# Sums over keys moved from TensorE to VectorE, and their reciprocals spread by DMA, in an attention and feed-forward kernel

## Chip, cores and metric

One core of one Trainium2 chip runs the kernel. The metric is the device time of one execution in microseconds. The kernel before takes 1441.41 us (median of 3 runs, 1440.82 to 1441.47).

## What is computed

The reference is an attention block followed by a feed-forward block, in float32 (the two weight matrices arrive as float64 and are turned into float32 by the kernel):

```python
# q, k, v: (8 batches, 12 heads, 448 rows, 64)
q_n, k_n = rmsnorm(q, g_q), rmsnorm(k, g_k)       # over the last axis
attn = softmax(q_n @ k_n.T / sqrt(64))            # over the keys
x = (attn @ v)  ->  (3584, 768)                   # batch*row, head*64
h = x @ w_in                                      # 768 -> 2048, "L1"
out = relu(h)**2 @ w_out                          # 2048 -> 768, "L2"
```

The softmax's denominator is the sum over keys of the exponentials, one number for each head and query. It is this sum, and its reciprocal, that the change computes in another way.

## The kernel before, in words

**Units of work.** Attention runs over pairs of heads: 8 batches times 6 pairs, 48 pairs in all, numbered i. The feed-forward block runs over four spans of two batches (12 pairs). Both of its matrix products are done by Strassen's scheme with seven products (in the code A11, S2, S1, S3, A12, A22, S4).

**Stages.** (1) The first 12 pairs run alone, in `attention_alone` (L814), while other engines turn the weights into float32 blocks and write them to DRAM (`prepare` L541, called through `weights` L619 in small ticks). (2) Then, for each span: the first product (`first_product` L893), and the second product (`second_product` L949), beside which the attention of the next span's 12 pairs runs (`attention` L844). There are three such stages of attention beside L2; the last span's second product runs alone.

**Order.** The schedule is written by hand: each engine executes its instructions in the order of the Python code, and waits on semaphores. `attention` is a generator that yields three times in each pair's iteration; after each yield the loop at L1058 to L1061 takes a share of the second product's steps (nearly all of one matmul each; 180 in a span, 160 of them beside attention). So the order of one iteration i is: loads of pair i+3 (`load` L656), scores of pair i for two of its four blocks of keys (`scores` L742), the values of pair i-1 (`values` L767), the other two blocks of scores, `finish(i-1)`; yield; two additions; `combine_x(i-1)`, load of v; yield; `transposes(i+1)`, `norm(i+2)`; yield.

**Steps of one pair beside L2, by engine and line.**
- TensorE: scores L748 (keys on partitions, queries along the free axis), values L772, sums L783, second product L973. A matmul of float32 gives two records in the trace. The two heads' values, of 64 output partitions each, go to the two halves of one PSUM tile, and so do the two heads' sums.
- ScalarE: the exponentials L755 (into one of six places in turn), the scaling of the transposed q by the gains L729, the squares for the normalisation L707.
- VectorE: the four blocks of exponentials are added up (L761, three additions on 112 partitions x 896), then, after TensorE's sum over partitions with a matrix of ones (L783, into the PSUM tile `tot`, each sum on 64 partitions), the reciprocal of `tot` L796 and the product with the values L797. Further the transposes of the next pair's q and k in squares of 32 (L728), and the sums for the normalisation (L710 to L715). It also takes the second product's results out of PSUM (L984 to L992), transposes them (L961), and forms Strassen's combinations of x (L807 to L812) and, in the first span, of the activations (L887 to L891).
- GpSimd: the power -0.5 of the normalisation (L716) and the two multiplications with it (L718).
- SyncE issues all DMAs of this stage: eight loads of q and k for a pair (L666, in the four quarters of 32 columns), two of v (L683), the stored blocks of w_out (`sw`, L648, five buffers), and four stores of each output tile (L964). The loads of pair i+3 overwrite the places from which `norm(i+1)` reads q and k.

**PSUM.** Scores have two tiles of two banks (`ps_s`), values and sums one bank each (`ps_o`, tags "o" and "t"), the second product two banks (`ps_m`).

The transposed q and k of a pair have a single place (`qkT[:, 0]`), so L728 for pair i+1 runs after pair i's last scores, and pair i+1's first scores wait for L728 and L729.

Of the kernel before, what the change touches and what calls it, by code (L numbers as in the profile page):

```python
# [386 lines left out]
def attention_then_ffn_bounded(  # L387
# [65 lines left out]
    ps_m = ctx.enter_context(tc.tile_pool(name="ps_m", bufs=2, space=bass.MemoryType.PSUM))  # L453

    qk, qkT, ident, mhalf, gains, rstd0, _ = held
    ones = consts.tile([SP, D], F32, name="ones")
    gT = consts.tile([P, NFC, 2 * S], F32, name="gT")
    xT = consts.tile([P, 2, NPAIR, S], F32, name="xT")
    xC = consts.tile([P, 3, HC, S], F32, name="xC")
# [190 lines left out]


    pts = {}
    vs, probs, pavs, tots, accs, normed, rstds = {}, {}, {}, {}, {}, {}, {0: rstd0}
    places = []

    def load(i):  # L656
        if i < NAT:
# [84 lines left out]
    def scores(i, c):  # L742

        at = i % 2 if i < NAT else 0
        sc = ps_s.tile([SP, 2, 512], F32, tag="s", name="sc")
        for h in range(2):
            rows = slice(h * D, (h + 1) * D)
            nc.tensor.matmul(sc[:, h, 0:S], qkT[rows, at, 1, c * SP:(c + 1) * SP], qkT[rows, at, 0, :],  # L748
                             start=True, stop=True)
        pr = probs[i, c] = places[(NJ * i + c) % len(places)]  # L750
        if i < NAT:
            for h in range(2):
                nc.scalar.activation(pr[:, h], sc[:, h, 0:S], AF.Exp, scale=rstds[i][:, 1, 2 * c + h:2 * c + h + 1])  # L753
        else:
            nc.scalar.activation(pr, sc[:, :, 0:S], AF.Exp)  # L755

    def add_up(work, i, c):

        if c == 1:
            accs[i] = work.tile([SP, 2, S], F32, tag="acc", name="acc", bufs=1)  # L760
        nc.vector.tensor_tensor(accs[i], probs[i, 0] if c == 1 else accs[i], probs[i, c], ALU.add)  # L761

    def places_for(work, n):

        places[:] = [work.tile([SP, 2, S], F32, tag=f"pr{m}", name="pr", bufs=1) for m in range(n)]

    def values(i, pe_sums):  # L767
        pavs[i] = ps_o.tile([P, S], F32, tag="o", name="pav")
        for c in range(NJ):
            pr = probs.pop((i, c))  # L770
            for h in range(2):
                nc.tensor.matmul(pavs[i][h * D:(h + 1) * D, :], vs[i][:, h, c, :], pr[:, h, :],  # L772
                                 start=(c == 0), stop=(c == NJ - 1))
            if pe_sums:
                sums(i, pr, c == 0, c == NJ - 1)
        if not pe_sums:
            sums(i, accs.pop(i), True, True)

    def sums(i, pr, first, last):
        if first:  # L780
            tots[i] = ps_o.tile([P, S], F32, tag="t", name="tot")
        for h in range(2):
            nc.tensor.matmul(tots[i][h * D:(h + 1) * D, :], ones, pr[:, h, :], start=first, stop=last)  # L783

    def finish(i):

        b, hp = divmod(i, NPAIR)
        tot, pav = tots.pop(i), pavs.pop(i)
        x = xT[:, b % 2, hp]
        if i < NAT:  # L790

            nc.vector.reciprocal(x.rearrange("d (p j) -> d j p", j=NJ), tot.rearrange("d (j p) -> d j p", j=NJ))
            x = x.rearrange("d (p j) -> d p j", j=NJ)
            pav = pav.rearrange("d (j p) -> d p j", j=NJ)
        else:
            nc.vector.reciprocal(x, tot)  # L796
        nc.vector.tensor_tensor(x, pav, x, ALU.mult)  # L797
        del vs[i]

# [14 lines left out]
    def attention_alone():  # L814


        for i in range(NAT):
            if i + 3 < NAT:
                load(i + 3)
            scores(i, 0)  # L820
            scores(i, 1)
            if i + 2 < NAT:
                norm(i + 2)
            elif i + 1 == NAT:
                norm(NAT)
                load(NAT + 2)
            if i:
                combine_x(i - 1)
            load_v(i + 1)
            if i + 1 < NAT:  # L830
                transposes(i + 1)
            scores(i, 2)
            scores(i, 3)
            if i + 1 < NAT:
                take_transposes(i + 1)
            yield
            values(i, True)
            finish(i)
            if i + 1 == NAT:
                combine_x(i)  # L840
            if NAT <= i + 3 < NAT + 2:
                load(i + 3)

    def attention(work, first):  # L844


        last = first + 2 * NPAIR
        for i in range(first, last + 1):
            if i + 3 < min(last + 2, B * NPAIR):
                load(i + 3)  # L850
            if i < last:
                scores(i, 0)
                scores(i, 1)
            if i == first:
                yield
            if i > first:
                values(i - 1, False)
            if i < last:
                add_up(work, i, 1)
                scores(i, 2)  # L860
                scores(i, 3)
            if i > first:
                finish(i - 1)
            yield
            if i < last:
                add_up(work, i, 2)
                add_up(work, i, 3)
            if i > first:
                combine_x(i - 1)
            if i < min(last, B * NPAIR - 1):  # L870
                load_v(i + 1)
            yield
            if i + 1 < last:
                transposes(i + 1)
            if i + 2 < last:
                norm(i + 2)
            yield
# [15 lines left out]
    def first_product(work, span):  # L893
# [11 lines left out]
        for f in range(HF):  # L905
# [1 line left out]
            g11, g12 = gT[:, f, 0:S], gT[:, f, S:2 * S]  # L907
            g21, g22 = gT[:, HF + f, 0:S], gT[:, HF + f, S:2 * S]
            add = nc.vector.tensor_tensor
            sums = {}  # L910
            for i in range(7):

                into, rhs = {A11: ("pa", B11), S2: ("pb", T2), S1: ("pc", T1), S3: ("pd", T3),
                             A12: ("pa", B21), A22: ("pd", T4), S4: ("pc", B22)}[i]
                first = into not in sums
                if first and into == "pa":
                    if span == 0 and f:
                        sums[into] = ps_o.tile([P, S], F32, tag="ot"[f % 2], name="pa")
                    else:
                        sums[into] = ps_s.tile([P, 2, 512], F32, tag="s", name="pa")[:, 0, 0:S]  # L920
                elif first:
                    sums[into] = ps_m.tile([P, S], F32, tag="m", name=into)
                ps = sums[into]
                load_blocks(n + i + 5)
                for c in range(HC):
                    nc.tensor.matmul(ps, stream[n + i][:, c], rhs[:, c], start=first and c == 0,  # L926
                                     stop=c == HC - 1, skip_group_check=not first)
                if i == A11:
                    p1 = work.tile([P, S], F32, tag="p1", name="p1")
                    nc.scalar.copy(p1, ps)  # L930
                elif i == S2:
                    z = work.tile([P, S], F32, tag="z", name="z")
                    add(z, p1, ps, ALU.add)  # L933
                elif i == S1:
                    y = work.tile([P, S], F32, tag="y", name="y")
                    add(y, z, ps, ALU.add)
                elif i == A12:
                    activate(g11, ps)
                else:
                    g, x = {S3: (g22, y), A22: (g21, z), S4: (g12, z)}[i]  # L940
                    add(g, x, ps, ALU.add)  # L941
                    activate(g, g)
                if span and f and i in (S1, A22):
                    combine(f - 1, (int(i == A22),))
                if span and f == HF - 1 and i == S4:
                    combine(f)
                yield

    def second_product(work, span):  # L949
# [17 lines left out]

        p1s, c11s = {}, {}
        for j, (m, i) in enumerate(uses2):
            ps = ps_m.tile([P, S], F32, tag="m", name="ps")  # L970
            for c in range(HF):
                load_blocks(n + 5)
                nc.tensor.matmul(ps, stream[n][:, c % 4], rhs_of[i][:, c], start=c == 0, stop=c == HF - 1)  # L973
# [28 lines left out]
    load_v(0)  # L1002
    nc.vector.memset(clamp1, 1151.0)
    nc.vector.memset(clamp2, 255.0 * 2.0 ** 23)
    nc.vector.memset(ones, 1.0)

    def ahead(u, nxt):

# [8 lines left out]
    with tc.tile_pool(name="words", bufs=2) as spare["pool"]:  # L1017
# [4 lines left out]
        norm(1)  # L1022
        with tc.tile_pool(name="first", bufs=2, reuse_waits="tile") as work:
            places_for(work, NJ)
            weights(4)
            for u, _ in enumerate(attention_alone()):


                weights(min(EARLY, 8 + (EARLY - 8) * (u + 1) // (NAT - 1)))
                if u == NAT - 2:  # L1030
                    load_blocks(5)
        with tc.tile_pool(name="first_product", bufs=2, reuse_waits="tile") as work:
# [11 lines left out]
    for span in range(NSPAN):  # L1044
# [7 lines left out]
        with tc.tile_pool(name="second_product", bufs=2, reuse_waits="tile") as work:  # L1052
            rest = second_product(work, span)
            if more:
                places_for(work, NJ + 1)
                places.append(qkT[:SP, 1])
                total, done = HC * (7 * HF + 4) - 20, 0
                for u, _ in enumerate(attention(work, nxt)):  # L1058
                    while done < min(total, total * (u + 1) // (6 * NPAIR + 1)):
                        next(rest)  # L1060
                        done += 1  # L1061
            for _ in rest:
# [90 lines left out]
```

## Time and profile before

| | us |
|---|---|
| median of 3 runs | 1441.41 |
| the profiled execution | 1440.65 |
| its span in the trace | 1439.2 |
| TensorE busy | 1416.6 |
| VectorE busy | 804.4 |
| GpSimd busy | 534.1 |
| ScalarE busy | 449.8 |
| `tot` matmuls beside L2 (L783), busy | 33.2 |
| reciprocals of `tot` beside L2 (L796), 36 of 2951 ns | 106.2 |
| additions of exponentials (L761), 96 of about 1.09 us | 117.9 |
| attention beside L2, three stages | 275 to 480, 620 to 822, 964 to 1166 |

The profile is that of one execution. A group of instructions has a line of the source, an engine, an operation, a shape and a count, its busy time and its mean; then the time for which the engine stood idle just before these instructions and what released it. "PEld" is TensorE's weight load. The time of DMAs is not the issuing engine's: "SPq" shows how long SyncE took to issue, and a median tells how long after that the data had landed.

### The profile page before, as it was taken

How to read it: one execution, taken by the hardware profiler on the slowest of the kernel's cores; microseconds unless marked ns; L12 is line 12 of the kernel's file. 1: busy time of each engine (PE TensorE's matmuls, PEld its weight loads, DVE VectorE, ACT ScalarE, POOL GpSimd, SP SyncE). 2: the span in 40 equal slices, each digit the busy share in tenths (PEclk: the TensorE clock that was granted, in tenths of full speed). 3: DMA queues.
4: the chain of work that ended last, by engine and by line, in shares of the span. 5: the costliest groups of instructions: out<-in, count | busy, mean ns of one | idle time of the engine just before them, and what ended most of it. 6: DMA issues, size and time to landing. Idle time of an engine off the chain costs nothing.

```text
span 1439.2 us, 14368 instructions
## 1 busy us (share of the span) xinstructions
PE 1416.6 (98%) x4662; PEld 654.4 (45%) x4662; DVE 804.4 (56%) x1163; ACT 449.8 (31%) x652; POOL 534.1 (37%) x367
## 2 busy tenths in 40 slices
PE   7999999999999999999999999999999999999997
PEld 3433454444444455444444455544444445555553
DVE  6778888478767433456666633355666652332111
ACT  6887687423323012133232111223323201110000
POOL 5877688333442022523444012433334302221000
PEclk9999999999999999999999999999999999999999
DMA  8576898644445333344454342343544333333443
GB/s 236 171 219 162 301 383 315 180 87 107 101 89 102 97 88 88 97 98 106 98 109 88 89 102 87 93 115 81 109 98 103 76 83 87 87 88 102 106 113 70
DMA packets 423639, 180.37 MB, mean 125 GB/s; under 512 B 274820, under 2 KB 421508, under 8 KB 423556
## 3 DMA queue, kind: packets, MB, share of 16 engines
q1 hardware_dynamic: 419716, 178.91, 47.4%
q10 hardware_dynamic: 3712, 0.46, 0.2%
q8 instruction: 39, 0.64, 0.2%
q14 instruction: 44, 0.36, 0.1%
q0 software_dynamic: 128, 0.00, 0.0%
HBM read 146.28 MB, written 33.03 MB: 125 GB/s over the span
## 4 chain that ended last, share of the span: by engine, by line
PE 92%; DVE 4%; DMA 2%; issue 1%; ACT 1%; POOL 0%; SPq 0%; DVEq 0%; POOLq 0%; ACTq 0%
PE ps L973 32%; PE sc L748 11%; PE pav L772 10%; PE pd L926 10%; PE pa L926 10%; PE pc L926 10%; PE pb L926 5%; PE tot L783 4%; DVE acc L761 1%; DVE xT L796 1%; DMA sw<-w1s 1%; PE pt L734 1%; DMA words<-in_moe_w_out_dram 0%; ACT qkT L729 0%; DMA vt<-in_v_dram 0%
## 5 line engine op out<-in xcount | busy, mean ns | idle before, releaser
L716 POOL TENSOR_TENSOR half<-half,mhalf 128x28 f32<-128x28 f32 x36 | 173.3, 4813 | 343.1 <-DVE half L715 343.1
L973 PE MATMUL ps<-gT,sw 128*128 128x448 f32 x768 | 299.1, 542 | 0.0
L903 POOL TENSOR_TENSOR gT<-gT 128x448 f32<-128x448 f32 x96 | 94.9, 990 | 372.9 <-ACT gT L899 372.9
L973 PE MATMUL ps<-gC,sw 128*128 128x448 f32 x576 | 225.2, 542 | 0.0
L973 PEld LDWEIGHTS ps<-gT,sw 128*128 128x128 f32 x768 | 143.9, 190 | 149.9 <-issue 146.5
L748 PE MATMUL sc<-qkT 64*112 64x448 f32 x768 | 171.3, 564 | 6.4 <-ACT pr L753 3.8
L755 ACT ACTIVATE pr<-sc 112x896 f32<-112x896 f32 x120 | 104.7, 914 | 200.8 <-PE sc L748 200.8
L973 PEld LDWEIGHTS ps<-gC,sw 128*128 128x128 f32 x576 | 108.0, 190 | 112.3 <-issue 111.7
L926 PE MATMUL pa<-xT,sw 128*128 128x448 f32 x384 | 155.0, 540 | 0.8 <-DMA sw<-w1s 0.8
L772 PE MATMUL pav<-pr,vt 112*64 112x448 f32 x672 | 146.0, 549 | 1.3 <-PE sc L748 1.3
L899 ACT ACTIVATE gT<-gT 128x448 f32<-128x448 f32 x96 | 55.2, 575 | 285.7 <-DVE gT L941 285.6
L796 DVE RECIPROCAL xT<-tot 128x448 f32<-128x448 f32 x36 | 106.2, 2951 | 19.3 <-PE tot L783 19.3
L748 PEld LDWEIGHTS sc<-qkT 64*112 64x112 f32 x768 | 60.4, 173 | 105.5 <-issue 71.8
L926 PEld LDWEIGHTS pa<-xT,sw 128*128 128x128 f32 x384 | 72.8, 190 | 72.7 <-issue 72.2
L772 PEld LDWEIGHTS pav<-pr,vt 112*64 112x64 f32 x672 | 44.5, 137 | 89.3 <-issue 75.5
L926 PE MATMUL pd<-xT,sw 128*128 128x448 f32 x192 | 78.0, 542 | 0.6 <-DVE z L933 0.5
L729 ACT ACTIVATE qkT<-qkT,gains 128x448 f32<-128x448 f32 x36 | 24.1, 668 | 174.0 <-DVE qkT L728 174.0
L926 PE MATMUL pb<-xC,sw 128*128 128x448 f32 x192 | 77.7, 540 | 0.4 <-DVE xC L810 0.4
L926 PE MATMUL pc<-xC,sw 128*128 128x448 f32 x192 | 77.4, 539 | 0.0
L926 PE MATMUL pd<-xC,sw 128*128 128x448 f32 x192 | 77.4, 539 | 0.0
L926 PE MATMUL pc<-xT,sw 128*128 128x448 f32 x192 | 77.4, 539 | 0.0
L941 DVE TENSOR_TENSOR gT<-z,pd 128x448 f32<-128x448 f32 x32 | 19.9, 622 | 101.5 <-PE pd L926 101.4
(119 smaller groups left out, 1608.6 us busy)
## 6 DMA issues: line engine op xcount, KB each, us to landing
sw<-w1s SPq DMA_DIRECT2D x224, 192.0 KB, 2.4
sw<-w2s SPq DMA_DIRECT2D x168, 256.0 KB, 3.2
w1s<-gC SPq DMA_DIRECT2D x8, 1344.0 KB, 6.8
w2s<-gC SPq DMA_DIRECT2D x8, 1344.0 KB, 7.7
out_dram<-osb SPq DMA_DIRECT2D x184, 56.0 KB, 1.9
qk<-in_q_dram SPq DMA_DIRECT2D x144, 56.0 KB, 2.2
qk<-in_k_dram SPq DMA_DIRECT2D x144, 56.0 KB, 2.2
vt<-in_v_dram SPq DMA_DIRECT2D x72, 112.0 KB, 3.2
```

What stands on the lines that cost most here:

```text
L716: nc.gpsimd.tensor_tensor(half, half, mhalf, ALU.pow)
L729: nc.scalar.activation(qkT[:, 0, 0], qkT[:, 0, 0], AF.Copy, scale=gains[:, 0:1])
L748: nc.tensor.matmul(sc[:, h, 0:S], qkT[rows, at, 1, c * SP:(c + 1) * SP], qkT[rows, at, 0, :], start=True, stop=True)
L755: nc.scalar.activation(pr, sc[:, :, 0:S], AF.Exp)
L772: nc.tensor.matmul(pavs[i][h * D:(h + 1) * D, :], vs[i][:, h, c, :], pr[:, h, :], start=(c == 0), stop=(c == NJ - 1))
L783: nc.tensor.matmul(tots[i][h * D:(h + 1) * D, :], ones, pr[:, h, :], start=first, stop=last)
L796: nc.vector.reciprocal(x, tot)
L899: nc.scalar.activation(g, src, AF.Relu)
L903: nc.gpsimd.tensor_tensor(g, g, g, ALU.mult)
L926: nc.tensor.matmul(ps, stream[n + i][:, c], rhs[:, c], start=first and c == 0, stop=c == HC - 1, skip_group_check=not first)
L941: add(g, x, ps, ALU.add)
L973: nc.tensor.matmul(ps, stream[n][:, c % 4], rhs_of[i][:, c], start=c == 0, stop=c == HF - 1)
```

## The change

In the three stages of attention beside L2:
- The matmuls with ones are left out (they stay in the first 12 pairs). Instead `fold(i)` on VectorE transposes the added-up exponentials in squares of 32, sums along the free axis, brings the four groups of partitions onto one and adds them, takes the reciprocal of the 2 x 448 sums (now 32 partitions x 28), transposes them and has SyncE store them in DRAM (3.5 KB, `factors`, two buffers). `spread(i)` issues two DMAs that read them back, each onto 64 partitions, into the place of `xT` where `finish` then multiplies. `finish` has no reciprocal there.
- `attention` yields four times in an iteration instead of three. `spread(i-1)` follows `values(i-1)`; `fold(i)`, `finish(i-1)` and `combine_x(i-1)` stand between the second and the third yield of the iteration; `transposes(i+1)` and `norm(i+2)` follow the third.
- The second product uses the freed bank (`ps_o`, tag "t") for every third of its tiles.

In the first 12 pairs the first four ticks of the weights' preparation are taken after pair 0's first scores and `norm(2)`, instead of ahead of pair 0.

```diff
+    def fold(i):
+        NG = S // 32
+        acc, quarters = sums["acc"].rearrange("p h q -> p (h q)"), sums["quarters"]
+        turned = places[NJ * (i + 1) % len(places)].rearrange("p h q -> p (h q)")
+        nc.vector.transpose(turned, acc)
+        nc.vector.tensor_reduce(quarters[:, 0], turned.rearrange("p (n k) -> p n k", k=32), AX, ALU.add)
+        for n in range(1, 4):
+            nc.vector.tensor_copy(quarters[0:32, n], quarters[n * 32:(n + 1) * 32, 0])
+        square, turned = sums["square"][:, 0], sums["square"][:, 1]
+        nc.vector.tensor_reduce(square[:, 0:2 * NG], quarters[0:32].rearrange("p a n -> p n a"), AX, ALU.add)
+        nc.vector.reciprocal(square[:, 0:2 * NG], square[:, 0:2 * NG])
+        nc.vector.transpose(turned, square)
+        nc.sync.dma_start(sums["out"][i % 2], turned[0:2 * NG])
+
+    def spread(i):
+        b, hp = divmod(i, NPAIR)
+        for h in range(2):
+            nc.sync.dma_start(xT[h * D:(h + 1) * D, b % 2, hp],
+                              sums["out"][i % 2].rearrange("(h g) t -> h () (g t)", h=2)[h].to_broadcast([D, S]))
...
     def finish(i):
...
-        else:
-            nc.vector.reciprocal(x, tot)
         nc.vector.tensor_tensor(x, pav, x, ALU.mult)
...
     def attention_alone():
...
             if i:
                 combine_x(i - 1)
+            else:
+                yield
             load_v(i + 1)
...
-    def attention(work, first):
+    def attention(first):
...
             if i > first:
-                values(i - 1, False)
+                values(i - 1)
+                spread(i - 1)
             if i < last:
-                add_up(work, i, 1)
+                add_up(i, 1)
                 scores(i, 2)
                 scores(i, 3)
-            if i > first:
-                finish(i - 1)
             yield
             if i < last:
-                add_up(work, i, 2)
-                add_up(work, i, 3)
-            if i > first:
-                combine_x(i - 1)
+                add_up(i, 2)
+                add_up(i, 3)
             if i < min(last, B * NPAIR - 1):
                 load_v(i + 1)
             yield
+            if i < last:
+                fold(i)
+            if i > first:
+                finish(i - 1)
+                combine_x(i - 1)
+            yield
             if i + 1 < last:
                 transposes(i + 1)
...
-            ps = ps_m.tile([P, S], F32, tag="m", name="ps")
+            ps = (ps_o.tile([P, S], F32, tag="t", name="ps") if j % 3 == 2
+                  else ps_m.tile([P, S], F32, tag="m", name="ps"))
...
-            weights(4)
-            for u, _ in enumerate(attention_alone()):
+            for u, _ in enumerate(attention_alone(), -1):
...
-                weights(min(EARLY, 8 + (EARLY - 8) * (u + 1) // (NAT - 1)))
+                weights(min(EARLY, 8 + (EARLY - 8) * (u + 1) // (NAT - 1)) if u >= 0 else 4)
...
-                for u, _ in enumerate(attention(work, nxt)):
-                    while done < min(total, total * (u + 1) // (6 * NPAIR + 1)):
+                for u, _ in enumerate(attention(nxt)):
+                    while done < min(total, total * (u + 1) // (8 * NPAIR + 1)):
```

The rest of the diff gives `acc`, `quarters` and `square` their tiles (the rows of `acc` from 112 on, and the unused columns of `square`, are set by GpSimd once in each stage), makes the six places 128 partitions tall, moves the matrix of ones into the first stage's memory, and renames.

## The prediction, made before the changed kernel had run

> **What bounds the kernel now.** I read the engines' busy time, then the table by stages for the three stages of attention beside L2, then SyncE's waits, then the timeline of one pair in the middle stage.
>
> ```profile
> PE 1416.6 (98%) x4662; PEld 654.4 (45%) x4662; DVE 804.4 (56%) x1163; ACT 449.8 (31%) x652; POOL 534.1 (37%) x367
> ```
>
> The three stages (their length, then busy time of TensorE, its weight load, VectorE, ScalarE and GpSimd, with counts; granted clock, DMA share, GB/s):
>
> ```profile
> 275.00:480.00 205.00, 203.44 (x733) 87.55 (x729) 147.78 (x218) 58.95 (x74) 67.91 (x30) 1.00 0.45 97
> 620.00:822.00 202.00, 201.88 (x728) 87.08 (x726) 131.85 (x189) 58.68 (x73) 70.46 (x31) 1.00 0.45 98
> 964.00:1166.00 202.00, 201.88 (x727) 87.02 (x727) 131.84 (x189) 58.04 (x72) 69.73 (x31) 1.00 0.42 92
> ```
>
> TensorE is full in all three stages, at full clock. VectorE has 65 to 72%, GpSimd 35%. So what TensorE is spared would be gained, if nothing else becomes late. What could is not in busy shares but in waits:
>
> ```profile
> SPq L666 <- POOL qk L718: 176.5, 30, 10.8
> ```
>
> Thirty times SyncE's queue stands still, 176.5 us in all, until GpSimd has read the places that the next loads of q and k overwrite. Today nothing urgent is queued behind. One round of it, by the timeline:
>
> ```profile
> 716.08 1.17 DVE L728 STREAM_TRANSPOSE qkT<-qk 128x448 f32<-128x448 f32 x2
> 716.75 0.67 ACT L729 ACTIVATE qkT<-qkT,gains 128x448 f32<-128x448 f32 x1 [6.11 <-DVE qkT L728]
> 718.29 1.09 DVE L710 TENSOR_REDUCE half<-qk 128x28 f32<-128x896 f32 x1 [1.05 <-ACT qk L707]
> 718.71 1.76 PE L748 MATMUL sc<-qkT 64*112 64x448 f32 x8
> 720.45 0.18 DVE L715 TENSOR_SCALAR half<-half 128x28 f32<-128x28 f32 x1
> 720.71 4.80 POOL L716 TENSOR_TENSOR half<-half,mhalf 128x28 f32<-128x28 f32 x1 [10.53 <-DVE half L715]
> 725.58 1.84 POOL L718 TENSOR_TENSOR qk<-qk,half 128x448 f32<-128x448 f32 x2
> 726.55 1.89 SPq L666 DMA_DIRECT2D qk<-in_q_dram  x4
> 728.49 0.62 DVE L797 TENSOR_TENSOR xT<-pav,xT 128x448 f32<-128x448 f32 x1
> 728.54 1.99 SPq L666 DMA_DIRECT2D qk<-in_k_dram  x4
> 730.62 0.52 SPq L648 DMA_DIRECT2D sw<-w2s  x1
> ```
>
> Transposes and normalisation of one pair on VectorE, then 4.80 us of powers on GpSimd, then eight loads on SyncE until 730.62. TensorE's next scores come at 735.22: a pair takes 16.51 us (718.71 to 735.22).
>
> [...] a load of q is issued in 0.47 us and lands 2.2 us after issue (median). [...] after 3.19 us idle at 17.29 us eight score records took 3.33 us instead of 1.76; after 2.41 us idle at 13.14 us nothing was slow.
>
> **The change, part by part.** The sum is made against the profiled execution (1440.65 us, span 1439.2), 0.76 below the median.
>
> *Removed on TensorE.* Per pair one sum of two heads: in the timeline it begins at 706.95 and the next scores at 707.80, of which 0.10 us is the change of shape that stays: 0.75 us. 36 pairs: 27 us. A pair needs 16.51 - 0.75 = 15.76 us of TensorE.
>
> *Removed and added on VectorE.* Removed 36 reciprocals of 2.95 us. `fold`, not in the trace: transpose of 896 columns as the two of L728, 1.17; sum like L710, 1.09; three copies like L713, 0.6; sum of 28 groups of 4, 0.26 (reductions of 512 and 1024 elements took 0.68 and 1.22, so 0.145 + 112 x 0.00105); reciprocal of 28 columns at 2951/448 ns, 0.2; small transpose 0.15; together 3.5 to 3.6 (bounds 3.2 and 4.2). So 0.6 more per pair, of no weight by itself at 65%.
>
> *Added on SyncE.* Three issues a pair, some 0.5 us each. The store waits for `fold`; behind it stand blocks of L2's weights, which in the built order are used a pair later, and q/k loads, which come after GpSimd anyway: nothing. 8 MB more beside 180 MB at 45% DMA share: nothing.
>
> *The new wait.* In the built program's order the two broadcasts stand directly behind the eight loads L666 on SyncE, and `finish` waits for them on VectorE. Behind `finish` stand `combine_x`, the taking out of L2's tiles, and the next pair's L728, L710 to L715; TensorE waits for L728 and L729. That closes a ring, from one pair's L728 to the next:
> - L728 to L710, through ScalarE: 716.08 to 718.29, 2.21
> - L710 to the end of L715, 720.63: 2.34
> - power and first multiplication, until the first load is issued at 726.55: 5.92
> - eight loads issued, until 730.62: 4.07
> - first broadcast's issue 0.5, second's landing 2.7: 3.2. Landing is the unknown: loads of 56 KB took 2.2, those of v (112 KB, the same size) 3.2; I take the middle, bounds 2.2 and 3.7
> - `finish`'s product to the next instruction (728.49 to 729.03): 0.54
>
> Sum 18.3 us (17.7 to 19.4), longer than TensorE's 15.76, and it holds no matmul of L2 that could hide it. Each 448-wide VectorE instruction between `finish` and L728 adds 0.54. Counted in the built order: 19 in stage one (combinations of the activations), 11 in stage two, 6 in stage three: 10.3, 5.9, 3.2 us.
>
> *Rounds.* The first broadcast is in a stage's second iteration, the last transposes in the tenth after the first: ten rounds. The last stage loads nothing for pairs past 47: eight. The first L728 of a stage has no `finish` before it. It follows the end of the first pair's scores by 2.5 us of additions and 3.6 of `fold`; the next scores follow L728 by 1.35 (717.42 plus a hop), and TensorE gets there only after 9.9 (625.5 to 635.42). So a stage begins with 2.45 us in hand; in the first, four combinations (2.1) leave 0.35. Between the second and twelfth scores:
> - stage one: 183 + 10.3 - 0.35 = 192.9, before 167.7 (290.30 to 457.97): +25.3
> - stage two: 183 + 5.9 - 2.45 = 186.4, before 166.0: +20.4
> - stage three, eight rounds to the tenth scores: 146.4 + 3.2 - 2.45 = 147.2, before 133.6: +13.6. Its next two pairs save 1.5 and lose about as much, because three combinations stand behind `fold`.
>
> The two sums at each stage's end are saved: 3 x 1.5 = 4.5. Net +54.8 us. TensorE's idle 2.5 us per pair may halve its clock for a while (1.6 us more work): 17.4 is still under 18.3, cost nothing; without that cover 28 x 1.6 = 45.
>
> *Third bank.* No matmul of L2 waited for a bank: nothing; it covers tiles taken out late behind `finish`.
>
> *The moved ticks.* ScalarE now takes pair 0's first exponentials at 10.8, but then pair 2's squares (L693), ahead of the ticks and of the other exponentials. That pair was issued from 7.83 on and landed 7.9 us after (median): about 16.7. From there, with the trace's durations: L693 to the end of the first L580 3.0, two activations 1.9, four exponentials 2.1, two copies 1.1, two activations 1.9, then as before 4.0 (24.58 to 28.55) to pair 0's reciprocal: 30.7, before 28.55. Pair 1's values waited for that pair's product (32.26 in the trace), and TensorE is full from there on: +2.2. Bounds: 3 us gained if the loads land 5 us earlier, 4 lost.
>
> Sum: 1440.65 + 54.8 + 2.2 = 1497.7; plus 0.76: 1498 us.
>
> **Rivals.**
> 1. *The ring is longer* (1528 us): 64 readers of one line of DRAM land after 3.8 us instead of 2.7, 28 rounds of 1.1. For it: the landing is not in the trace. Against: only 3.5 KB are read again and again.
> 2. *The ring is shorter* (1462 us): loads issued or landing faster, 17.0 per round. Against: 0.47 us per issue in all of 80 loads.
> 3. *The ring doesn't bind* (1428 us, faster). One mechanism: the broadcast has landed before `fold` ends, some 6.1 us after a pair's last scores, so that only VectorE's queue sets L728. Then 27 us are saved, 2 lost at the start, and 12 where four combinations or three stand between `fold` and L728 (five pairs of stage one at about 1.5, the last ones at 1 to 2): 1441.4 - 27 + 2 + 12. It decides where a round falls below 16.3 us (18.3 - 57/28). For it: before, the loads were often all issued by 3 us after the scores (712.43 against 709.49). Against: there VectorE was early; once L728 is at the edge, everything behind it moves along.
> 4. *No change to be measured*: the ring near 16.3 by chance. That the sums are still on TensorE is excluded: the built program has none beside L2.
>
> **How the numbers follow.** Forecast 0.70 (1478 to 1520), longer 0.14, shorter 0.09, not binding 0.05, no change 0.02. A measurement of this kernel tells some 0.2% from no change. Faster 0.05, same 0.02, slower 0.93. The range: the ring's bounds, 28 x -0.6 and 28 x +1.1, and the start's give about 1474 to 1531.
>
> **What would show it.** Right: `tot` only in the first 12 pairs; SyncE's wait for L718 about as before; `finish`'s product released by the DMA of `xT`, two to four us idle each, 28 to 34 times; scores (L748) released by L729 with two to three us idle per pair; stages of about 220 us. Each hop of the ring can be read off. Wrong: `finish` running without a wait for a DMA, or TensorE full in the stages. At the start, L693 earlier than 16 us would refute the last term.

## The result, and the profile after

The changed kernel takes 1545.47 us (median of 4 runs, 1542.91 to 1548.23), the kernel before beside it 1441.44: a ratio of 1.0721 [1.0699, 1.0743]. The side was forecast, the size was not: 1498 us was predicted, and 1545 lies 14 us above the range's upper end.

Engines and granted clock (in tenths of full speed, by fortieths of the span) in the page of the changed kernel:

```profile
PE 1433.2 (93%) x4518; PEld 655.7 (42%) x4518; DVE 840.1 (54%) x1415; ACT 452.5 (29%) x652; POOL 544.6 (35%) x373
PEclk9999999999998999999999899999999999999999
```

TensorE has 144 matmul records fewer (the 36 pairs' sums), yet is busy 16.6 us longer, in a span of 1546.4 us instead of 1439.2. The three stages of attention beside L2, each now whole (length; busy time of TensorE, weight load, VectorE, ScalarE, GpSimd; clock; DMA share; GB/s):

```profile
279.40:524.00 244.60, 211.55 (x691) 89.00 (x691) 163.18 (x303) 60.55 (x74) 73.53 (x33) 0.93 0.41 93
662.40:903.00 240.60, 210.39 (x692) 88.62 (x692) 145.47 (x275) 59.67 (x73) 73.14 (x34) 0.94 0.42 95
1040.90:1276.00 235.10, 209.07 (x693) 88.44 (x693) 147.02 (x275) 59.97 (x73) 73.85 (x34) 0.94 0.40 93
```

Before, TensorE was full and its clock 1.00. Now it stands idle for 26 to 33 us in each stage, and some of the rest runs at half clock (0.50 from 754.12 to 757.45, below; the mean granted clock is 0.93 to 0.94). No other engine is nearly full: VectorE has 60 to 67%. So it is waits. SyncE's, and then the other engines' (who waits, for whom; us in all, times, longest):

```profile
SPq L666 <- POOL qk L718: 207.9, 30, 10.9
SPq L776 <- DVE square L775: 59.8, 21, 6.7
```

```profile
PE sc L748 <- ACT qkT L729: 89.3, 30, 5.2
DVE xT L821 <- DMA xT<-factors: 40.2, 18, 4.5
DVE ct L1020 <- PE ps L1003: 137.0, 31, 10.7
DVE y L1017 <- PE ps L1003: 44.0, 9, 6.5
```

TensorE's wait is the predicted one: scores wait for the scaling of the transposed q and k, 30 times. But only 18 of 36 finishes waited for the broadcast, where 28 to 34 had been foretold. And VectorE waits far longer than before for L2's tiles (the same two places had 91.3 and 16.2 us).

Where the time came from, by first scores of pairs (L748), in us:

| stretch | before | predicted | after |
|---|---|---|---|
| start of the first stage | 273.7 | +2.2 | 279.4 |
| stage one, second to twelfth scores | 167.7 | 192.9 | 205.2 |
| stage two, the same | 166.0 | 186.4 | 201.1 |
| stage three, second to tenth scores | 133.6 | 147.2 | 155.4 |
| stage three, tenth to twelfth scores | 32.5 | 32.5 | 39.7 |
| all the rest (changes alone) | | -4.5 | -0.1 |

The differences add up to the 107.2 us of the two spans. Two neighbouring rounds of stage two show what the sum had missed. The first, from one pair's transposes (L728) to the next pair's:

```profile
732.72 1.16 DVE L728 STREAM_TRANSPOSE qkT<-qk 128x448 f32<-128x448 f32 x2
737.35 4.79 POOL L716 TENSOR_TENSOR half<-half,mhalf 128x28 f32<-128x28 f32 x1 [11.95 <-DVE half L715]
742.22 2.79 POOL L718 TENSOR_TENSOR qk<-qk,half 128x448 f32<-128x448 f32 x2
744.14 1.89 SPq L666 DMA_DIRECT2D qk<-in_q_dram  x4
746.13 1.99 SPq L666 DMA_DIRECT2D qk<-in_k_dram  x4
748.08 0.20 DVE L775 STREAM_TRANSPOSE square<-square 32x32 f32<-32x32 f32 x1
748.16 1.13 SPq L782 DMA_DIRECT2D xT<-factors  x2
752.19 0.62 DVE L821 TENSOR_TENSOR xT<-pav,xT 128x448 f32<-128x448 f32 x1 [3.91 <-DMA xT<-factors]
752.73 1.16 DVE L728 STREAM_TRANSPOSE qkT<-qk 128x448 f32<-128x448 f32 x2
```

This is the predicted ring through SyncE: `fold` ends at 748.28 and VectorE then waits 3.91 us for the broadcast, which stood behind eight loads, which stood behind GpSimd. 20.0 us, where 18.3 (18.9 with this stage's instructions behind `finish`) was the sum. The next round:

```profile
754.12 3.33 PE L748 MATMUL sc<-qkT 64*112 64x448 f32 x8 [3.43 <-ACT qkT L729]
761.79 1.76 PE L748 MATMUL sc<-qkT 64*112 64x448 f32 x8
763.48 5.53 PE L1003 MATMUL ps<-gT,sw 128*128 128x448 f32 x14
765.12 1.09 DVE L760 TENSOR_TENSOR acc<-acc,qkT 112x896 f32<-112x896 f32 x1
767.21 1.13 SPq L782 DMA_DIRECT2D xT<-factors  x2
769.05 0.62 DVE L1020 TENSOR_TENSOR ct<-y,ps 128x448 f32<-128x448 f32 x1 [2.83 <-PE ps L1003]
770.12 1.10 DVE L768 STREAM_TRANSPOSE pr<-acc 128x896 f32<-128x896 f32 x1
773.69 0.20 DVE L775 STREAM_TRANSPOSE square<-square 32x32 f32<-32x32 f32 x1
773.83 0.57 DVE L821 TENSOR_TENSOR xT<-pav,xT 128x448 f32<-128x448 f32 x1
774.33 1.15 DVE L728 STREAM_TRANSPOSE qkT<-qk 128x448 f32<-128x448 f32 x2
```

Here `finish` waits for nothing: the broadcast was out early. What is late is `fold` itself. The sum was complete at 766.2, but VectorE's queue holds an L2 tile ahead of `fold` (L1020), TensorE begins on that tile only after its scores, and so `fold` starts at 770.12, 17.4 us after L728, and ends at 773.89. This is a second ring: L728, scores, values, scores, L2 tile, `fold`, `finish`, L728. It took 21.6 us, and TensorE's half clock after its idle 3.43 us (granted clock 0.50 from 754.12 to 757.45: 3.33 us for eight score records, not 1.76) lies on it.

### The profile page after: what moved, and what is told of

It reads as the page before. It is cut to its first block, busy times and chain, and to the rows that moved or that the text cites. A ratio compares the mean times of both kernels' runs of the same rounds, so it can differ in the third digit from the quotient of the medians.

```text
span 1546.4 us, 14545 instructions
## 1 busy us (share of the span) xinstructions
PE 1433.2 (93%) x4518; PEld 655.7 (42%) x4518; DVE 840.1 (54%) x1415; ACT 452.5 (29%) x652; POOL 544.6 (35%) x373
## 4 chain that ended last, share of the span: by engine, by line
PE 59%; issue 21%; DVE 7%; DMA 4%; POOL 3%; ACT 3%; SPq 2%; POOLq 0%; DVEq 0%; ACTq 0%
PE ps L1003 16%; PE pd L955 9%; PE pa L955 8%; PE pc L955 8%; PE sc L748 7%; PE pav L804 6%; PE pb L955 4%; PE tot L807 2%; POOL qk L718 2%; SPq L666 1%; DVE acc L760 1%; DMA sw<-w1s 1%; DMA xT<-factors 1%; DVE quarters L769 1%; DVE pr L768 1%
## 5 line engine op out<-in xcount | busy, mean ns | idle before, releaser
L748 PE MATMUL sc<-qkT 64*112 64x448 f32 x768 | 196.2, 634 | 91.1 <-ACT qkT L729 89.3
L804 PE MATMUL pav<-pr,vt 112*64 112x448 f32 x672 | 159.5, 589 | 7.4 <-ACT pr L753 4.2
L748 PEld LDWEIGHTS sc<-qkT 64*112 64x112 f32 x768 | 66.6, 190 | 198.4 <-ACT qkT L729 111.7
L760 DVE TENSOR_TENSOR acc<-acc,pr 112x896 f32<-112x896 f32 x60 | 74.8, 1247 | 66.8 <-ACT pr L755 64.1
L804 PEld LDWEIGHTS pav<-pr,vt 112*64 112x64 f32 x672 | 48.6, 150 | 116.0 <-issue 97.0
L718 POOL TENSOR_TENSOR qk<-qk,half 128x448 f32<-128x448 f32 x72 | 79.6, 1126 | 2.8
```

The source lines that it names most:

```text
L718: nc.gpsimd.tensor_tensor(qkn[:, s], raw[:, s], half[:, s * NG:(s + 1) * NG].rearrange("p g -> p g ()").to_broadcast([P, NG, 32]), ALU.mult)
L760: nc.vector.tensor_tensor(acc, probs[i, 0] if c == 1 else acc, probs[i, c], ALU.add)
```

## The experiments

The theory: two rings, through SyncE (S) and through `fold` (F), each longer than TensorE's 15.76 us per pair, and whichever is longer sets a round. The rivals: S alone, mis-sized; TensorE's half clock as the cause; the start; the third bank. All medians are of 4 runs unless another number stands there; the kernel before took 1441.3 to 1441.6 beside them. Edits are to the changed kernel.

**1. The start undone.** The first ticks of the weights go back ahead of the first 12 pairs.

```diff
-            else:
-                yield
...
-            for u, _ in enumerate(attention_alone(), -1):
+            weights(4)
+            for u, _ in enumerate(attention_alone()):
...
```

> The changed kernel with the first four ticks of the weights' preparation put back ahead of pair 0; all else as changed. In the changed trace the attention beside L2 begins 5.6 us later than before (279.38 against 273.74). Theory (the moved ticks make it late): 1540 us, 5 to 6 below the changed kernel, and the first stage begins at about 274 again. Rival (the start is late by chance or by the matrix of ones being set later): no change, 1545.

1541.64 us, 1.0691 [1.0673, 1.0709]: 3.8 us less than the changed kernel. The first stage began at 274.60 instead of 279.38. That is one execution of each, and this start varies: in the eight traces of changed kernels that keep the moved ticks it lies at 275.6 to 279.5 (mean 277.4), in the five that undo them at 273.6 to 276.4 (mean 274.8). So the start costs some 2.6 (by the means) to 3.8 us (by the medians). The loss lies elsewhere.

**2. S cut.** The broadcasts of pair i-1 are issued ahead of the loads, not behind them.

```diff
         for i in range(first, last + 1):
+            if i > first:
+                spread(i - 1)
             if i + 3 < min(last + 2, B * NPAIR):
                 load(i + 3)
...
                 values(i - 1)
-                spread(i - 1)
```

> The changed kernel with the two broadcasts issued at the top of the iteration, ahead of the eight loads of q and k, instead of behind them; VectorE's order is unchanged. This cuts the ring through SyncE's queue. Theory of two rings (the second goes from L728 through the next scores, the values, the exponentials, the additions, L2's tiles and fold to the next L728, and is lengthened only where TensorE has fallen to half clock): without the first ring [...] a pair takes 16 to 17 us, 1430 to 1455 us. Theory of the one ring, as predicted: everything is given back, 1420. Rival (fold on VectorE's path is the cause, and the broadcast only coincides): 1530 or more.

1502.48 us, 1.0429 [1.0412, 1.0446]. Waits of this run:

```profile
PE sc L748 <- ACT qkT L729: 59.9, 26, 4.3
DVE xT L821 <- DMA xT<-factors: 11.8, 3, 4.7
```

The broadcast is waited for 3 times, not 18, each time at a stage's end, with no scores behind it; yet scores still wait 26 times, and the time is 61 us over the kernel before. S alone as the cause falls: without it, F holds the rounds (15.4 to 21.6 us, with `fold` starting 10.7 to 16.2 us after L728 and `finish` directly behind it). Both expectations were too low, since F was taken for the shorter ring.

**3. No half clock.** Two matmuls more (1.5 us), whose result is overwritten, fill TensorE's idle time ahead of each pair's first scores beside L2.

```diff
+        for h in range(2 if i >= NAT and c == 0 else 0):
+            nc.tensor.matmul(sc[:, h % 2, 0:S], ident[:, 0:SP], gT[:, h, 0:S], start=True, stop=True)
```

> The changed kernel with two further matmuls of 128 x 112 x 448 on TensorE (1.5 us) directly ahead of each pair's first scores beside L2, into the tile that the scores then overwrite; they wait for nothing late. So TensorE has 54 us more work, in the place where it stands idle for 3 us on average. Theory of two rings with the half clock: the idle time falls to 1.5 us, the clock stays up, the rounds fall from 20.1 to about 18.7, 1500 to 1520 us, faster than the changed kernel although it does more. Rival (the clock has no part in it, a round is only SyncE's ring and longer than thought): 1545, unchanged, the work lies in the idle time. Rival (TensorE's work is on the path): 1545 + 54 = 1599.

1545.69 us, 1.0727 [1.0709, 1.0745]: no gain, though the clock over the run rose from 0.966 to 0.984 and only 8 of the 36 pairs' first scores were still slowed, where it had been 21.

```profile
PE sc L750 <- ACT qkT L729: 57.3, 24, 5.1
DVE xT L823 <- DMA xT<-factors: 50.2, 22, 4.8
```

Broadcast waits went up to 22 (50.2 us): where F became shorter, S took its place. So the half clock is not what decides, while S stands. How much it adds where F binds stays open, since the filling also takes TensorE's time.

**4. L728 taken out of both rings.** The next pair's transposes and normalisation go ahead of `finish` and `fold` in VectorE's queue, and `finish` ahead of `fold`.

```diff
             yield
-            if i < last:
-                fold(i)
-            if i > first:
-                finish(i - 1)
-                combine_x(i - 1)
-            yield
             if i + 1 < last:
                 transposes(i + 1)
             if i + 2 < last:
                 norm(i + 2)
             yield
+            if i > first:
+                finish(i - 1)
+                combine_x(i - 1)
+            if i < last:
+                fold(i)
+            yield
```

> The changed kernel with the next pair's transposes and normalisation on VectorE ahead of fold, finish and combine_x, instead of behind them; SyncE's order of broadcasts and loads is unchanged. L728 then waits neither for the broadcast nor for fold: both rings are cut. Theory (the order on VectorE is all that costs): TensorE is full in the three stages, 36 x 0.75 = 27 us are gained, 5.6 lost at the start: 1420 to 1430 us. Rival (the broadcast or its store is slow in itself, or SyncE's queue delays L2's weights): still above 1500.

1431.73 us, 0.9940 [0.9923, 0.9957]: all of the loss is gone and the kernel is a little faster than before, with the broadcasts still behind the eight loads and `fold` itself unchanged. SyncE even stands 169.7 us for `fold`'s result before it stores it, where it was 59.8 in the changed kernel, so that wait was not the loss either. What is left, in this run's waits:

```profile
PE pav L804 <- DVE xT L821: 9.0, 10, 2.1
PEld pav L804 <- DVE xT L821: 19.8, 15, 2.8
```

`finish` is now late for the single PSUM bank of the values.

**5. `fold` alone earlier**, directly behind the additions, SyncE's order unchanged.

```diff
                 add_up(i, 2)
                 add_up(i, 3)
+                fold(i)
...
             yield
-            if i < last:
-                fold(i)
             if i > first:
```

> The changed kernel with fold issued directly behind the last addition, one yield earlier, so that no tile of L2 stands ahead of it on VectorE; SyncE's order is unchanged. This shortens the second ring (fold behind a tile that TensorE finishes only 4 to 6 us after the scores) and leaves the first through SyncE. Theory of two rings: the first alone remains, rounds of 18.6 to 20, 1500 to 1525 us. Rival (the second ring is an effect of the first): no gain, 1545. Rival (the second is all): below 1460.

1535.64 us, 1.0647 [1.0629, 1.0665]: 9.8 less, a smaller gain than expected; experiment 6 shows why.

**6. Experiments 2 and 5 together.**

> Fold directly behind the last addition, and the broadcasts ahead of the eight loads on SyncE: the first ring cut, the second shortened to 1.4 + 6.5 + 2.7 + 3.8 + 0.55 us plus what stands between finish and L728, 15 to 17 us against TensorE's 15.76. Theory of two rings: 1425 to 1450 us. Rival (a third delay is hidden behind the two): 1480 or more.

1488.3 us, 1.0320 [1.0303, 1.0338]. Far off what was expected. The timeline of a round says why:

```profile
752.12 2.52 PE L1003 MATMUL ps<-gC,sw 128*128 128x448 f32 x6
754.68 0.62 DVE L1020 TENSOR_TENSOR ct<-p,ps 128x448 f32<-128x448 f32 x1 [4.42 <-PE ps L1003]
755.21 2.46 DVE L760 TENSOR_TENSOR acc<-acc,pr 112x896 f32<-112x896 f32 x2
757.70 1.11 DVE L768 STREAM_TRANSPOSE pr<-acc 128x896 f32<-128x896 f32 x1
```

The tile that VectorE waits for (4.42 us) stands ahead of the last two additions, as it does in some rounds of the changed kernel too (5.16 us at 409.10 there): after the first yield of an iteration L2's steps are queued, and the additions follow the yield. Moving `fold` to the additions didn't take the tile out of F.

**7. The next pair first, and everything else.** Transposes, then `fold`, directly behind the additions; after the yield `norm`, then `finish`; with 1 and 2.

```diff
                 add_up(i, 3)
+            if i + 1 < last:
+                transposes(i + 1)
+            if i < last:
+                fold(i)
...
             yield
-            if i < last:
-                fold(i)
+            if i + 2 < last:
+                norm(i + 2)
             if i > first:
                 finish(i - 1)
                 combine_x(i - 1)
             yield
-            if i + 1 < last:
-                transposes(i + 1)
-            if i + 2 < last:
-                norm(i + 2)
             yield
```

> The next pair's transposes directly behind the last addition, then fold; the normalisation ahead of finish; broadcasts ahead of the loads; the first ticks back ahead of pair 0. Everything that was late is then early. Theory: TensorE is full in the three stages, 27 us less of 1441.4: 1412 to 1420 us.

1439.01 us (18 runs), 0.9981 [0.9974, 0.9989]; some 20 more than expected. The values wait for `finish` (22.1 us, and 42.7 of their weight loads), which frees their bank: it stands behind `fold` and `norm`, and starts 17.8 us after a pair's first scores, where it was 16.3 in 4 (medians).

**8. The same with two banks for L2.**

```diff
-            ps = (ps_o.tile([P, S], F32, tag="t", name="ps") if j % 3 == 2
-                  else ps_m.tile([P, S], F32, tag="m", name="ps"))
+            ps = ps_m.tile([P, S], F32, tag="m", name="ps")
```

> As e7_next_first_all, with two banks for the second product instead of three. Theory (no matmul of L2 waits for a bank): the same as e7 within 2 us. Rival (tiles are taken out late behind fold on VectorE, and the third bank covers it): 5 to 20 us more than e7.

1438.3 us (10 runs), 0.9973 [0.9964, 0.9983], the intervals of 7 and 8 overlap: in the order of 7 the third bank is worth nothing that can be measured. In the changed kernel's own order it was not tried.

**9. F shortened, S as it was.** The last two additions and `fold` go ahead of the first yield, so that no tile stands before them.

```diff
                 scores(i, 2)
                 scores(i, 3)
-            yield
-            if i < last:
                 add_up(i, 2)
                 add_up(i, 3)
+                fold(i)
+            yield
...
             yield
-            if i < last:
-                fold(i)
             if i > first:
```

> The changed kernel with the last two additions and fold issued on VectorE directly behind the pair's scores, ahead of the first yield, so that no tile of L2 (which VectorE would wait 3 to 5 us for) stands ahead of them; SyncE's order unchanged. In e5 and e6 such a tile still stood ahead of the additions. Theory (ring through SyncE, and a second ring whose size is VectorE's wait for L2's tile): the SyncE ring alone remains, rounds of 18.3 to 19.5, 1500 to 1525 us. Rival (the tile's wait is not the term): as e5, 1535.

1527.91 us, 1.0613 [1.0584, 1.0642], 3 above the expected stretch. The broadcast is now waited for 22 times, not 18, and such a round is S alone:

```profile
738.67 1.11 DVE L768 STREAM_TRANSPOSE pr<-acc 128x896 f32<-128x896 f32 x1
742.25 0.20 DVE L775 STREAM_TRANSPOSE square<-square 32x32 f32<-32x32 f32 x1
746.78 0.62 DVE L821 TENSOR_TENSOR xT<-pav,xT 128x448 f32<-128x448 f32 x1 [3.83 <-DMA xT<-factors]
```

`fold` has ended by 742.45, and `finish` waits 3.83 us for the broadcast. This is what the prediction had described. The kernel takes 30 us more than the prediction said; but F is not gone from it: in a third of the rounds `finish` still follows `fold` without a wait for the broadcast.

**10. Experiments 2 and 9 together**: S cut, F shortened.

> As e9_adds_early, and the broadcasts ahead of the eight loads on SyncE as in e2. Theory (these two are all): the second ring shrinks to some 15 to 16.5 us, TensorE's 15.76 decides, 1422 to 1440 us. Rival (the tile's wait is not the term): as e6, 1488.

1464.56 us, 1.0162 [1.0142, 1.0183]. Better than either alone, but 25 above the expected stretch. One round:

```profile
707.99 2.84 DVE L760 TENSOR_TENSOR acc<-acc,pr 112x896 f32<-112x896 f32 x2 [2.54 <-ACT pr L755]
710.93 1.11 DVE L768 STREAM_TRANSPOSE pr<-acc 128x896 f32<-128x896 f32 x1
714.64 0.57 DVE L1013 TENSOR_TENSOR p<-p,ps 128x448 f32<-128x448 f32 x1
715.14 0.60 DVE L821 TENSOR_TENSOR xT<-pav,xT 128x448 f32<-128x448 f32 x1
715.67 1.15 DVE L728 STREAM_TRANSPOSE qkT<-qk 128x448 f32<-128x448 f32 x2
```

No wait for a tile or a broadcast is left in it, and from the last L728 (699.38) it still takes 16.3 us: scores, values, scores, additions, `fold` and `finish` in a row. Even the bare ring F, 15.4 to 17.8 us at full clock in stages two and three, is mostly longer than TensorE's 15.76. So L728 should not stand behind `fold` here.

**11. The best version.** Experiment 10, with the next pair's transposes between additions and `fold`, `finish` ahead of `norm`, and the start undone.

```diff
...
                 scores(i, 3)
-            yield
-            if i < last:
                 add_up(i, 2)
                 add_up(i, 3)
+                if i + 1 < last:
+                    transposes(i + 1)
+                fold(i)
+            yield
             if i < min(last, B * NPAIR - 1):
                 load_v(i + 1)
-            yield
-            if i < last:
-                fold(i)
             if i > first:
                 finish(i - 1)
                 combine_x(i - 1)
             yield
-            if i + 1 < last:
-                transposes(i + 1)
             if i + 2 < last:
                 norm(i + 2)
+            yield
             yield
...
```

> As e10, with the next pair's transposes between the additions and fold, finish ahead of the normalisation, and the first ticks back ahead of pair 0. Theory: TensorE waits for nothing in the three stages, 27 us are gained: 1412 to 1422 us. Rival (VectorE's queue, at some 85% of a pair of 15.76 us, makes something else late): 1425 to 1440.

1411.44 us, 0.9787 [0.977, 0.9803]: the fastest of all, 30 us under the kernel before. Its page and one iteration on VectorE:

```profile
PE 1389.8 (98%) x4518; PEld 643.5 (46%) x4518; DVE 839.6 (59%) x1415; ACT 450.8 (32%) x652; POOL 555.6 (39%) x373
```

```profile
699.97 0.63 DVE L728 STREAM_TRANSPOSE qkT<-qk 128x448 f32<-128x448 f32 x1
700.88 0.65 DVE L728 STREAM_TRANSPOSE qkT<-qk 128x448 f32<-128x448 f32 x1 [0.28 <-POOL qk L718]
701.45 1.07 DVE L768 STREAM_TRANSPOSE pr<-acc 128x896 f32<-128x896 f32 x1
704.99 0.20 DVE L775 STREAM_TRANSPOSE square<-square 32x32 f32<-32x32 f32 x1
705.12 0.57 DVE L821 TENSOR_TENSOR xT<-pav,xT 128x448 f32<-128x448 f32 x1
```

L728 runs as soon as the additions behind the scores are done, `fold` and `finish` behind it, where nobody on TensorE waits for them. TensorE is full again: eleven pairs of stage two follow each other in 174.1 us, 15.83 each, where it was 182.6 and 16.60 before.

**12. Experiments 4, 2 and 1 together**, the other way to take L728 out.

> e4_next_first (1431.7) with the broadcasts ahead of the loads and the first ticks back ahead of pair 0. In e4 VectorE waited six times for the broadcast, 23.3 us, and TensorE 29 us in all for finish. Theory: 4 us from the start and up to 15 from these waits, 1412 to 1427. Rival (finish is late for fold's and L2's tiles' sake): 1428, the start's 4 us alone.

1422.93 us, 0.9872 [0.9855, 0.9888], inside the expected stretch. Between 4 and 11: `finish` behind `norm` is still late for the values' bank (7.7 us, and 17.2 of weight loads).

The runs that matter, side by side (us):

| | S as changed | S cut |
|---|---|---|
| F as changed | 1545 | 1502 |
| F shortened | 1528 | 1465 |
| L728 out of F and S | 1432 (4) | 1423 (12), 1411 (11) |

Experiments 11 and 12 also have the start undone. Cutting S is worth 43 with F as it was, and 63 with F shortened; shortening F is worth 18 with S as it was, and 38 with S cut. Each saves more once the other is out of the way, as it must where the longer of two sets each round. With neither in L728's way, the sign turns.

## Why the prediction was right or wrong

**TensorE's share: right.** 0.75 us per pair was to be saved, 15.76 to be left. Experiment 11 shows pairs of 15.83 us in the mean, 15.76 the commonest; its span is 27.0 us shorter than that of the kernel before (1412.2 against 1439.2), its median 30. Third bank at nothing: not contradicted (8, in another order).

**The ring through SyncE: right in its path, too short in its terms.** Hop by hop from L728, predicted and then as the changed kernel's rounds had it:
- first load issued: 10.47; 10.45 in some rounds, 11.42 in others. In the latter GpSimd's first multiplication L718 lay beside the additions L760 on VectorE: the two multiplications take 2.79 above (742.22) instead of 1.84. In this trace L718 takes 0.94 us (median) and up to 1.90, L760 1.09 and up to 1.87. The 17 of 72 L718 that took over 1.0 us each overlapped an L760, and the 21 of 108 L760 that took over 1.15 each overlapped an L718; 17 more L718 overlapped an L760 and took no more than 0.94. Why some are lengthened and others not is not shown. The trace of before had shown it too (lines below): two multiplications in 2.69 us beside an addition of 1.39, while the round used for the sum, with 1.84, was one without
- broadcasts issued: 14.54; 14.48 or 15.44
- `finish`: 17.74; 17.9 to 19.7. Issue 0.58 each and landing 2.8 us (2.6 to 4.7) instead of 0.5 and 2.7

```profile
707.49 2.69 POOL L718 TENSOR_TENSOR qk<-qk,half 128x448 f32<-128x448 f32 x2
707.99 1.39 DVE L761 TENSOR_TENSOR acc<-pr 112x896 f32<-112x896 f32 x1 [4.92 <-PE tot L783]
```

With `fold` earlier (9) the kernel takes 1527.91, 30 above the prediction. In its trace the start is no part of that (275.6, 1.9 late where 2.2 was predicted). The rounds of the three stages took 25.4 more than the sum had, and all the rest 3.6 more. The longer hops are in the 25.4, and so are the rounds of F that are left in 9; how they share it was not worked out.

**The step that failed** is in rival 3: that `fold` ends "some 6.1 us after a pair's last scores", and so lies beside the ring. In the second round above the scores ended at 763.5 and `fold` at 773.9, 10.3 later; over the 36 pairs it was 6.4 to 10.3, the median 9.1. The 6.1 were additions and `fold` as if VectorE's queue held nothing between them. But what stands in a queue ahead counts: an L2 tile, whose matmuls TensorE only starts behind those scores; in stage one also four combinations of 0.6 each (287.8 to 290.2). Where the prediction's sum has L2's tiles, behind `finish`, they cost 0.54 us each with no wait for their matmuls; the tile ahead of `fold` above waited 2.83. So `fold`, whose 0.6 us of work more per pair were "of no weight by itself", closed a second ring. What experiment 9 takes out of that ring is worth 17.6 us with S as it was (1545.47 - 1527.91), and 37.9 where S is cut (1502.48 - 1464.56). That 17.6 and the 30 are the 47 us that the prediction was short.

**TensorE's half clock at no cost: the reason was too narrow, the cost is open.** The 17.4 us under 18.3 looked at TensorE's work alone; on F the scores are a hop, and from L728 to their end a round needs 9.4 to 10.9 us at half clock instead of 8.0. Experiment 3 found no gain from a higher clock while S stands, as predicted; its share on F isn't settled.

**Stage ends: wrong.** Each stage's last two sums were to save 1.5 us. The twelfth pair's first scores ran at half clock (granted 0.52 and 0.54 in stages two and three: 3.24 us, not 1.76), which takes back 1.5; in all 2 us were lost from there on. The rounds before a stage's second scores gave 2.2 back, so that the last row of the table is -0.1, not -4.5. And the last two pairs of stage three, put at nothing, lost 7.3: F binds there, with no load of q or k left on SyncE.

**The start: right in its cause, near in its size.** Lines of the changed kernel:

```profile
17.41 1.06 ACT L693 ACTIVATE qk<-qk 112x1024 f32<-112x1024 f32 x1 [5.35 <-DMA qk<-in_k_dram]
22.90 2.28 PE L804 MATMUL pav<-pr,vt 112*64 112x448 f32 x4 [4.22 <-ACT pr L753]
31.18 2.95 DVE L818 RECIPROCAL xT<-tot 128x448 f32<-128x448 f32 x1
```

L693 at 17.41 (predicted 16.7) and the reciprocal at 31.18 (30.7) are as worked out: ScalarE sits idle 5.35 us for the loads of pair 2. Left out was that TensorE then waits 4.22 us in the middle of pair 0's values and goes on at half clock (granted 0.50). The first stage started 5.6 late in this execution, not 2.2; the means over the traces (1) are 2.6 apart, and undoing it gave back 3.8.

**The range** took in the bounds of the landing and the start, but no second ring: the only case with `fold` in it was on the fast side. From its own terms (landing 2.2 to 3.7 us, start 3 gained to 4 lost) come 1479 to 1528 rather than 1474 to 1531; the result lies above either.

## What to carry to other kernels

Where work is moved off a full engine onto an in-order queue (here SyncE's: the broadcasts were issued at 748.16, behind the eight loads begun at 744.14), write down every closed path from an instruction back to itself in the next round, through each queue with all that stands ahead in it, and compare each sum with the full engine's share; one such ring found is no proof that it is the only one. What the full engine waits for (here L728) belongs ahead of new work that nobody waits for (`fold`, `finish`): with L728 moved, the same change went from 7.2% slower to 0.6% faster (4), and with the other moves of 11 to 2.1% faster. A hop's price should be taken from several rounds of a trace, the long ones too, not from the one that reads most cleanly.

## What the runs showed of the hardware

- VectorE's additions of 112 x 896 (L760) and GpSimd's multiplications of 128 x 448 (L718), both float32, took longer in many of the places where they overlapped: up to 1.87 us instead of 1.09, and up to 1.90 instead of 0.94 (medians).
- The length of the idle time alone did not settle whether the clock fell to half: in the changed kernel eight score records took 1.76 us after 2.04 us of idleness and 3.33 (granted clock 0.50) after 2.71; after 2.25 they took 1.76 once and 2.58 and 2.85 at other times, and after 2.94 they took 2.09 at one place (775.71) and 3.32 at another (1152.43).
- Small VectorE instructions took longer than large ones scaled down: a reciprocal of 32 x 28 took 0.32 us and a sum of 32 x 112 0.33, where 0.2 and 0.26 had been worked out; `fold` took 3.77 in all (770.12 to 773.89).
- A broadcast of one DRAM line of 1792 bytes to 64 partitions landed 2.8 us after its issue (median), no slower than the loads of v, which move as much (3.0 us).
